# A new order for the first quarter of a fused RWKV and mixture-of-experts kernel, with filler matmuls at other places

## The chip, the cores and the metric

The kernel runs on one core of a Trainium2 chip. Its engines have a queue each: TensorE (PE, with its weight loads as PEld), VectorE (DVE), ScalarE (ACT), GpSimd (POOL), and SyncE (SP), which issues all loads and stores here. The metric is the device time of one execution in microseconds, as the median of several runs.

## The reference

Inputs are `r, k, v, w` of shape (batch 4, heads 8, sequence 768, head size 48), `u` (8 x 48), and the weights of 4 experts (`wq, wk, wv` 384 x 64 each, `wo` 64 x 384) with a gate (384 x 4).

```python
for t in range(S):
    cur = np.einsum('bhd,bhe->bhde', u[None] * kt, vt)
    y[:, :, t] = np.einsum('bhd,bhde->bhe', rt, state + cur)
    state = wt[:, :, :, None] * state + np.einsum('bhd,bhe->bhde', kt, vt)
...
logits = x @ w_gate                       # x: y with the heads side by side (384)
topk = np.argpartition(-logits, K, axis=-1)[..., :K]      # K = 2, softmax over the two: w
for e in range(E):
    q, k, v = x @ wq[e], x @ wk[e], x @ wv[e]
    scores = np.where(causal, -1e9, scale * (q @ k.transpose(0, 2, 1)))
    a = softmax(scores)
    out += (mask of e in topk) * w * (a @ v @ wo[e])
```

## The kernel before

The work is cut into eight units `(b, g)`: batch entry `b`, first or second half `g` of its 768 steps. Each unit has two parts.

`rwkv(b, g)` turns the recurrence into matrix products over chunks of 64 steps. The heads are taken in four pairs. Per pair, the running products of the decays `w` are made by scans on DVE (`suf`, `pre`), after a product of neighbouring decays (`w2`). Keys and rows are scaled with them (`kw`, `rw`, `kt`, `mr`). PE transposes the scaled keys (`ktp`), ACT copies them (`kts`), and PE multiplies them with the values (`ups`). From these the state goes on chunk by chunk, on DVE (`ws`, line 468; the first step of unit 0 on ACT, `us`, line 470). PE also makes the products of keys and rows inside a chunk (`aps`); they are masked with the decay mask `dec_mask` on their way out (`am`). The output `yps` is the sum of both, and DVE adds it into `xn` (`addy`). In unit 0 the term of `u` has its own products: `rkp` on DVE or POOL, and `rkm`, PE products with only two columns. For unit 0 pairs are handled one by one (names with a last digit 0 to 3, or `0000`, `0001`, `0020`, `0021`), for later units two by two.

`moe(b, g)` transposes `xn` (`xp`), makes Q, K and V (`proj`, `vproj`), the scores (`sc`), minimum and exponential (`max` on DVE, `exp` on ACT), the transposes of these (`tp`, `ev`), the product with V (`av`), the gate and the output product.

Every step is one entry that `plan.add` records. Which engine takes a step, and in which order each engine meets its steps, is not found by a scheduler at build time: the string `ORDER` has one word for each step, the engine's letter (A ACT, V DVE, P PE, G POOL, S SP) and the step's number. Each engine runs its words strictly in this order. A load (S) is also made to wait for the last PE step that stands ahead of it in the list, so the list paces the loads.

Among the steps are 94 warming products (numbers 8 to 101, line 1054), matmuls of 128 x 512 bf16 whose result nobody reads. A step whose number stands in no word is left out, so the list also says how many warming products there are and where. Each takes one of the eight PSUM banks (`ps`); PE meets it in order, and it waits until the last reader of the bank's former content is done.

The decay mask and the causal mask are made once, by `masks3` (step V2, lines 329 and 330) and `masks2` (step V3, line 333); `masks4` (V4) makes `tri` and a one-hot table.

## Time and profile before

| | |
|---|---|
| median of 3 runs | 308.04 us (307.08 to 311.17) |
| profiled execution | 308.01 us, span 306.1 us |
| granted PE clock, mean of the span | 0.989 |
| busy share PE, DVE, ACT, POOL | 97%, 81%, 73%, 51% |
| DMA traffic | 44.09 MB, mean 144 GB/s |
| share of PE in the chain that ended last | 93% |

Busy time of PE counts an instruction until its modelled end, so an engine that is always busy may still run at half its clock; the granted clock (1.00 is 2.4 GHz, 0.50 is 1.2 GHz) has to be read beside it. Two per cent of the time are 6.2 us.

### The profile page before, as it was taken

Reading aid. Unit: us, or ns where it says so; the run is one execution under the profiler, and the core shown is the slowest. Engines: PE = TensorE matmul, PEld = TensorE weight load, DVE = VectorE, ACT = ScalarE, POOL = GpSimd, SP = SyncE. Lnnn points to the kernel's source line nnn. Section 1 sums busy time; section 2 is a strip of 40 time slices with the busy share of each in tenths; the row PEclk is TensorE's granted clock in tenths of the full one; section 3 lists DMA queues with packets and bytes.
Section 4 is the critical chain, followed back from the end, with each engine's and each line's share of the span. In section 5 each row is a group of like instructions: output and inputs, shape, how many; then the busy total and the mean of one; then the engine's idle time right before and its main releaser. Section 6 shows DMA issues by size and latency. Waiting matters only on the chain.

```text
span 306.1 us, 12703 instructions
## 1 busy us (share of the span) xinstructions
PE 295.6 (97%) x5216; PEld 245.0 (80%) x5216; DVE 248.1 (81%) x703; ACT 222.0 (73%) x688; POOL 155.3 (51%) x247
## 2 busy tenths in 40 slices
PE   7879999899999999999999999999999999999995
PEld 2669669778886897999789778898889977898784
DVE  5987999989999999989898997978587644687652
ACT  4336399988999889889899867464788656649852
POOL 4848597928556548267787769634211101210510
PEclk9995999999999999999999999999999999999999
DMA  7976785881649763656671573010100000000212
GB/s 227 359 277 216 255 277 167 292 300 43 212 134 329 222 208 117 218 163 207 206 232 77 173 271 107 6 41 24 51 28 2 0 28 28 2 26 2 79 62 94
DMA packets 20073, 44.09 MB, mean 144 GB/s; under 512 B 2352, under 2 KB 10032, under 8 KB 20016
## 3 DMA queue, kind: packets, MB, share of 16 engines
q1 hardware_dynamic: 20016, 43.29, 42.8%
q8 instruction: 41, 0.67, 0.9%
q14 instruction: 16, 0.13, 0.1%
HBM read 38.56 MB, written 4.72 MB: 141 GB/s over the span
## 4 chain that ended last, share of the span: by engine, by line
PE 93%; DVE 3%; issue 1%; DMA 1%; SPq 0%; ACT 0%; DVEq 0%; ACTq 0%
PE ps L779 16%; PE ps L929 13%; PE ps L881 12%; PE ps L1000 9%; PE ps L261 9%; PE ps L817 8%; PE ps L686 5%; PE ps L257 4%; PE ps L399 4%; PE ps L401 4%; PE ps L445 3%; PE ps L772 3%; PE ps L811 1%; DMA lt<-in_wkr_dram 1%; PE ps L978 1%
## 5 line engine op out<-in xcount | busy, mean ns | idle before, releaser
L897 ACT ACTIVATE a<-a,mx 128x128 f32<-128x128 f32 (+5 forms) x96 | 63.8, 667 | 10.0 <-DVE mx L892 9.6
L892 DVE CUSTOM_DVE_ANT_0 a<-ps,causal 128x256 f32<-128x256 f32 (+5 forms) x96 | 56.4, 619 | 12.2 <-PE ps L881 10.8
L265 ACT COPY AT<-ps 128x512 f32<-128x512 f32 (+5 forms) x74 | 38.6, 546 | 10.1 <-PE ps L261 7.9
L929 PE MATMUL ps<-AT,v_sb 128*64 128x384 f32 (+2 forms) x308 | 40.4, 405 | 0.1
L468 DVE CUSTOM_DVE_ANT_0 ys<-ps,ys,suf 112x48 f32<-112x48 f32 x144 | 33.4, 262 | 3.2 <-PE ps L445 0.4
L929 PEld LDWEIGHTS ps<-AT,v_sb 128*64 128x64 f32 x308 | 20.0, 136 | 16.5 <-issue 12.2
L664 ACT ACTIVATE xn<-nat,rk 128x48 f32<-128x48 f32 x126 | 30.5, 326 | 2.0 <-DVE rk L656 1.9
L779 PE MATMUL ps<-xh,wh_qk 128*128 128x384 f32 x84 | 30.4, 362 | 0.0
L881 PE MATMUL ps<-K,Q 64*128 64x384 f32 (+4 forms) x160 | 30.2, 415 | 0.0
L779 PE MATMUL ps<-xl,wh_qk 128*128 128x384 f32 x84 | 28.4, 338 | 0.1
L779 PE MATMUL ps<-xh,wl_qk 128*128 128x384 f32 x84 | 28.3, 336 | 0.0
L989 POOL TENSOR_TENSOR yl<-yr,yh 128x384 fp32r<-128x384 f32 x13 | 13.1, 1010 | 27.5 <-ACT yh L988 26.3
L399 PE MATMUL ps<-vy,am 64*64 64x48 f32 x768 | 25.8, 225 | 1.3 <-issue 1.3
L261 PEld LDWEIGHTS ps<-ident,a 64*128 64x128 f32 x560 | 23.1, 138 | 4.4 <-issue 1.6
L261 PE MATMUL ps<-ident,a 64*128 64x64 f32 x560 | 26.3, 225 | 0.1
L401 PE MATMUL ps<-ys,pre 48*64 48x48 f32 x704 | 25.5, 224 | 0.0
L636 POOL TENSOR_TENSOR kt<-lt,suf 128x768 f32<-128x768 f32 x13 | 21.9, 1685 | 6.3 <-DVE kr L643 3.5
L401 PEld LDWEIGHTS ps<-ys,pre 48*64 48x64 f32 x704 | 22.9, 138 | 2.2 <-DVE wend L464 1.1
L399 PEld LDWEIGHTS ps<-vy,am 64*64 64x64 f32 x768 | 23.5, 139 | 0.1
L638 POOL TENSOR_TENSOR pre<-lt,w 128x768 f32<-128x768 f32 x11 | 18.6, 1690 | 9.6 <-DVE w L630 5.4
L686 PE MATMUL ps<-pre,kt 48*64 48x64 f32 x768 | 18.3, 227 | 1.4 <-issue 0.7
L693 DVE TENSOR_TENSOR am<-ps,dec_mask 64x384 f32<-64x384 f32 (+1 forms) x33 | 18.2, 552 | 1.4 <-PE ps L686 1.0
(173 smaller groups left out, 823.2 us busy)
## 6 DMA issues: line engine op xcount, KB each, us to landing
lt<-in_wkr_dram SPq DMA_DIRECT2D x28, 384.0 KB, 4.4
kr<-in_nat_dram SPq DMA_DIRECT2D x14, 576.0 KB, 4.2
lt<-in_wkr_dram SPq DMA_DIRECT2D x14, 397.0 KB, 4.4
nat<-in_nat_dram SPq DMA_DIRECT2D x16, 288.0 KB, 3.9
vy<-in_vY_dram SPq DMA_DIRECT2D x32, 144.0 KB, 3.7
out_dram<-ob SPq DMA_DIRECT2D x24, 192.0 KB, 1.9
lt<-in_wkr_dram SPq DMA_DIRECT2D x3, 583.0 KB, 5.8
w_qk<-in_wqk_dram SPq DMA_DIRECT2D x1, 768.0 KB, 8.0
```

Of the source, the lines that this page charges most:

```text
L261: nc.tensor.transpose(o()[:, h * 512 + i * 64:h * 512 + i * 64 + 64], src[r], ident[r, r])
L265: nc.scalar.copy(o, i)
L399: nc.tensor.matmul(to, am()[k, c, :], vy()[k, c, :], start=zero and x == 0, stop=i == 2 and x == len(group) - 1)
L401: nc.tensor.matmul(to, pre()[r, c, :], ys()[r, c, :], start=i == x == 0, stop=False)
L468: nc.vector._custom_dve(TENSOR_TENSOR_REDUCE_ADD_MIN, out=new, in0=inc, in1=old, s0=3.0e38, s1=by)
L664: nc.scalar.mul(to[:, i, h, :], v()[:, i, h, :], rk()[:, i, h:h + 1])
L686: nc.tensor.matmul(apss[x]()[half(h if first else h ^ x), c * C:(c + 1) * C], kt()[r, c, :], pre()[r, c, :], start=True, stop=True)
L779: nc.tensor.matmul(pp()[:, 0:384], w[:, qk, k, cs], x()[:, k, :], start=(k == j == 0), stop=(k == j == 2))
L881: nc.tensor.matmul(spv(x)[:, h, :], q_()[p, t], flat(k_())[p, o], start=j == 0, stop=j == len(terms) - 1)
L892: nc.vector.tensor_tensor_reduce(out=a()[:, 0:n].rearrange("p (a n) -> p a n", a=np_), in0=spv(x), in1=causal[:, S - n:S].rearrange("p (a ...
L897: plan.add("exp", {"ACT": t_exp(n)}, lambda e, x=x, y=y, mx=mx, a=a: nc.scalar.activation(a()[:, 0:n], a()[:, 0:n], AF.Exp, bias=mx(), sca ...
L929: nc.tensor.matmul(yp()[e * 64:e * 64 + 64, lo:hi], v_sb()[:, j, ep * 128 + e * 64:ep * 128 + e * 64 + 64], at, start=(j == 0), stop=(j == ...
```

## The change

The change replaces the first two dozen lines of `ORDER`, up to the middle of the first batch entry's second half (the scores of unit `(0, 1)` on PE). From there on the list is as before, but for one load that has another place. Nothing else in the file is touched. All steps of the reference's arithmetic remain. Fourteen steps go to another engine: among them three small copies and a row sum from ACT to DVE, a product of decays of 397 columns from POOL to DVE, one of 576 columns from POOL to DVE, and two of 384 columns from DVE to POOL. Of the warming products 20 stand in the list instead of 21. The first lines of the table, as the diff has them (a row of numbers says little by itself):

```diff
 ORDER = """
-A0 V4 S113 V123 V124 A1 V126 S114 S115 S116 A5 A125 V120 G128 S6 S117 P79 S176 P53 P28 P9 P68 P88 P10 G129 V3 S177 P94
...
+V4 S113 V2 S114 V3 V123 A0 V124 V126 S115 S6 V120 V125 S116 S117 G128 P23 V127 V130 G129 V145 V131 P34 S176 P68 P71
...
```

The queue of PE from its first instructions on. Before, twelve warming products (`causal` is their input) run ahead of the first transposes of keys (`kt000`), then five more and the key sums (`nat000`, `kts0000`), and the products of the `u` term (`rkm`, from `kr000`) come only behind these:

```order
L445 MATMUL ps_68<-nat000_129,kts0000_180 48x48 x12
L1054 LDWEIGHTS causal_69
L1054 MATMUL ps_68<-causal_69 128x512
L570 MATMUL ps_68<-u_t_90,kr000_125 128x2 x3
L257 MATMUL ps_68<-ident_80,kt000_150 128x128 x3
L570 MATMUL ps_68<-u_t_90,kr000_125 128x2 x3
L1054 LDWEIGHTS causal_69
L1054 MATMUL ps_68<-causal_69 128x512
L445 MATMUL ps_68<-nat000_129,kts0001_212 48x48 x12
```

Now four warming products stand ahead of the first `rkm`, then two, and then the transposes, with three more behind them:

```order
L1054 MATMUL ps_68<-causal_69 128x512
L570 MATMUL ps_68<-u_t_90,kr000_124 128x2 x3
L1054 LDWEIGHTS causal_69
L1054 MATMUL ps_68<-causal_69 128x512
L1054 LDWEIGHTS causal_69
L1054 MATMUL ps_68<-causal_69 128x512
L257 MATMUL ps_68<-ident_80,kt000_134 128x128 x3
```

What moved: `rkm` of pair 0 went from behind the second pair's transposes to the front, and eight of the first twelve warming products are gone from there.

The queue of DVE at its start, from the one-hot table on. Before, the masks come late: `causal` behind the first `kr` product, and `dec_mask` only ahead of the scan of the third pair (`w2002`):

```order
L338 TENSOR_SCALAR tri_100<-tri_100 128x16
L578 TENSOR_TENSOR w2000_114<-lt0_66 128x199
L623 SCALAR_TENSOR_TENSOR ps_68<-w2000_114,ps_68 128x198
L628 RECIPROCAL ps_68<-ps_68 128x6
L563 TENSOR_TENSOR kr000_125<-lt0_66 128x2x192
L333 TENSOR_SCALAR causal_69<-d128_78 128x128
L630 SCALAR_TENSOR_TENSOR ps_68<-w2000_114,ps_68 128x198
```

```order
L638 TENSOR_TENSOR pre000_155<-lt0_66,ps_68 128x2x192
L329 TENSOR_SCALAR dec_mask_99<-d128_78 64x64
L330 TENSOR_SCALAR dec_mask_99<-d128_78 64x64
L623 SCALAR_TENSOR_TENSOR ps_68<-w2002_178,ps_68 128x198
L468 ISA ys0000_195<-ps_68,ys0000_195,suf000_123 112x48
```

Now:

```order
L338 TENSOR_SCALAR tri_100<-tri_100 128x16
L329 TENSOR_SCALAR dec_mask_99<-d128_78 64x64
L330 TENSOR_SCALAR dec_mask_99<-d128_78 64x64
L333 TENSOR_SCALAR causal_69<-d128_78 128x128
L578 TENSOR_TENSOR w2000_116<-lt0_66 128x199
L623 SCALAR_TENSOR_TENSOR ps_68<-w2000_116,ps_68 128x198
L628 RECIPROCAL ps_68<-ps_68 128x6
L563 TENSOR_TENSOR kr000_124<-lt0_66 128x2x192
L267 COPY suf000_126<-ps_68 128x6
L630 SCALAR_TENSOR_TENSOR ps_68<-w2000_116,ps_68 128x198
```

What moved: all three mask operations went ahead of the first product of decays (`w2000`), and a copy of six columns came from ACT.

The queue of PE behind the outputs of the first two pairs (`vy0000`, `am0000`), down to the key sums of the fourth pair (`kts0021`). Before, one warming product stands there:

```order
L399 MATMUL ps_68<-vy0000_197,am0000_289 64x48 x4
L1054 LDWEIGHTS causal_69
L1054 MATMUL ps_68<-causal_69 128x512
L257 MATMUL ps_68<-ident_80,xn00_323 128x128 x3
L257 MATMUL ps_68<-ident_80,kt010_350 128x128 x6
L570 MATMUL ps_68<-u_t_90,kr002_363 128x2 x6
L257 MATMUL ps_68<-ident_80,kt002_376 128x128 x3
L445 MATMUL ps_68<-nat010_241,kts0100_380 48x48 x20
L445 MATMUL ps_68<-nat002_217,kts0021_399 48x48 x12
```

Now two stand behind the outputs, and one behind each of the next small groups:

```order
L1054 MATMUL ps_68<-causal_69 128x512
L257 MATMUL ps_68<-ident_80,xn00_311 128x128 x3
L257 MATMUL ps_68<-ident_80,kt010_344 128x128 x6
L1054 LDWEIGHTS causal_69
L1054 MATMUL ps_68<-causal_69 128x512
L570 MATMUL ps_68<-u_t_90,kr002_347 128x2 x3
L1054 LDWEIGHTS causal_69
L1054 MATMUL ps_68<-causal_69 128x512
L257 MATMUL ps_68<-ident_80,kt002_365 128x128 x3
L570 MATMUL ps_68<-u_t_90,kr002_347 128x2 x3
L1054 LDWEIGHTS causal_69
L1054 MATMUL ps_68<-causal_69 128x512
```

What moved: three warming products came in between, the two `rkm` of the second two pairs are parted, and the long key sums of unit `(0, 1)` (`kts0100`) went behind those of the first unit. Three more warming products, where there was one, stand between the `aps` of the first two pairs and their outputs.

## Rows read from the trace of the kernel before

**Rows 1.** Busy time by stretch: stretch, each engine's busy us (records), clock, DMA.
```profile
20.25:23.66 3.41, 3.19 (x84) 2.74 (x84) 3.38 (x9) 2.27 (x7) 1.78 (x3) 1.00 0.30 93
23.66:30.48 6.82, 6.64 (x168) 6.27 (x168) 4.77 (x19) 4.00 (x12) 5.62 (x5) 0.50 0.75 241
30.48:76.00 45.52, 44.50 (x794) 34.73 (x797) 42.01 (x123) 36.18 (x129) 32.43 (x38) 1.00 0.68 224
76.00:306.10 230.10, 226.03 (x3960) 191.89 (x3951) 182.51 (x512) 172.62 (x523) 103.09 (x177) 1.00 0.34 111
```

**Rows 2.** The same view in slices of 1 us, at the clock's two edges.
```profile
23.00:24.00 1.00, 1.00 (x52) 0.89 (x40) 1.00 (x3) 1.00 (x3) 0.49 (x1) 0.83 0.05 17
...
30.00:31.00 1.00, 1.00 (x8) 0.59 (x6) 0.52 (x2) 0.00 (x0) 1.00 (x3) 0.76 0.26 86
```

**Rows 3.** Timeline of PE: start, duration, line, operation [idle before, and its releaser].
```profile
1.42 5.30 PE L1054 MATMUL ps<-causal 128*128 128x512 bf16 x12 [1.42 <-POOL causal L285]
7.38 0.55 PE L257 MATMUL ps<-ident,kt 128*128 128x128 f32 x3 [0.66 <-DVE kt L636]
7.77 1.24 PE L1054 MATMUL ps<-causal 128*128 128x512 bf16 x5
...
10.62 0.73 PE L570 MATMUL ps<-u_t,kr 128*128 128x2 f32 x6
...
11.52 0.48 PE L445 MATMUL ps<-nat,kts 64*48 64x48 f32 x24
...
15.04 0.38 PE L1054 MATMUL ps<-causal 128*128 128x512 bf16 x1 [0.84 <-DVE ys L468]
...
18.57 0.20 PE L399 MATMUL ps<-vy,am 64*64 64x48 f32 x1 [1.28 <-issue]
```

**Rows 4.** Timeline of DVE, the same columns.
```profile
3.41 0.36 DVE L578 TENSOR_TENSOR w<-lt 128x199 f32<-128x199 f32 x1
...
5.49 0.56 DVE L563 TENSOR_TENSOR kr<-lt 128x384 f32<-128x384 f32 x1 [0.81 <-DMA lt<-in_wkr_dram]
5.97 0.22 DVE L333 TENSOR_SCALAR causal<-d 128x128 bf16<-128x128 f32 x1
...
10.10 0.16 DVE L267 COPY suf<-ps 128x6 f32<-128x6 f32 x1
10.17 0.54 DVE L638 TENSOR_TENSOR pre<-lt,ps 128x384 f32<-128x384 f32 x1
10.63 0.67 DVE L329 TENSOR_SCALAR dec_mask<-d 64x64 f32<-64x64 f32 x1
...
11.90 0.57 DVE L623 TENSOR_TENSOR_SCAN ps<-w,ps 128x198 f32<-128x198 f32 x1
...
18.81 0.46 DVE L412 TENSOR_TENSOR xn<-ps,kr 128x288 f32<-128x288 f32 x1 [0.86 <-PE ps L399]
...
23.52 0.55 DVE L634 TENSOR_TENSOR lt<-lt 128x384 f32<-128x384 f32 x1
...
25.68 0.56 DVE L693 TENSOR_TENSOR am<-ps,dec_mask 128x384 f32<-128x384 f32 x1 [0.66 <-PE ps L686]
26.49 0.92 DVE L468 CUSTOM_DVE_ANT_0 ys<-ps,ys,suf 112x48 f32<-112x48 f32 x4 [0.26 <-ACT ys L470]
...
27.89 0.56 DVE L693 TENSOR_TENSOR am<-ps,dec_mask 128x384 f32<-128x384 f32 x1 [0.17 <-PE ps L686]
...
30.48 0.46 DVE L412 TENSOR_TENSOR xn<-ps,kr 128x288 f32<-128x288 f32 x1 [0.82 <-PE ps L399]
...
36.15 0.76 DVE L643 TENSOR_TENSOR kr<-kr 128x576 f32<-128x576 f32 x1
...
36.95 0.81 DVE L656 TENSOR_REDUCE rk<-kr 128x6 f32<-128x288 f32 x2
```

**Rows 5.** Timeline of ACT: the first copy of transposed keys and the first state.
```profile
7.97 0.48 ACT L265 COPY kts<-ps 128x384 f32<-128x384 f32 x1 [3.08 <-PE ps L257]
9.52 0.30 ACT L470 ACTIVATE ys<-ps,suf 112x48 f32<-112x48 f32 x1 [1.08 <-PE ps L445]
```

More of the change, by code (lines that the diff above doesn't have):

```diff
@@ new lines @@
+V146 V148 G142 V147 V149 S177 G150 P121 P94 A122 P100 P133 G151 A134 V152 S119 P88 V153 P83 P56 G184 S118 P135 A136
+V137 S243 V185 V186 P143 P81 V187 A5 A144 V138 G154 P155 P52 V188 V139 P25 S244 A156 S102 G206 P157 A158 V159 S246
+V160 V140 A1 V161 G132 V141 V162 S180 P165 A168 P164 P55 P39 S178 V207 V163 V209 V210 G169 V166 P42 A251 G250 V252 S7
+A274 P173 V174 P170 V171 S245 A208 V253 P41 V254 G255 S292 G257 P73 V203 P237 P265 V181 V211 S179 S107 A105 V213 P96
+P182 A103 A266 G212 V183 V189 P24 G190 A238 P216 V214 P204 V191 G193 V192 A268 P62 A217 V256 G258 G106 S287 P218 A219
@@ new lines @@
+V220 A205 V221 V222 S288 G294 G104 S340 G347 G299 P194 P225 V227 A195 P196 A197 V198 V199 V223 P267 V200 A108 V224
+V201 P226 V229 V202 V275 S289 P231 V232 V276 V269 P234 A215 V235 S247 P967 V295 S248 S249 S341 V296 V270 P241 G300
+S290 A242 P239 A240 V297 V271 V272 P280 V273 S342 V277 V278 A312 P971 V298 P968 P969 V281 A348 V259 V260 V263 A318
+P916 V261 A970 P920 P921 P922 S291 P917 G301 V279 A262 G302 P912 V283 P918 P913 A919 S384 V923 P914 A915 P309 P937
+P946 A310 G352 V349 V350 V351 V940 A941 A392 V938 S386 V949 A950 P311 G353 V947 A264 P955 V313 V319 V956 P944 S385
@@ new lines @@
+V958 V314 A945 V320 P972 V315 V321 V316 G303 V322 G304 V305 V317 A959 V307 G354 S343 P924 P973 A974 S344 P953 G391
+A954 V323 P324 V325 G397 V327 V393 A939 A948 A308 P285 V286 A957 P975 P925 P926 A306 G355 S293 P928 P929 P930 V976
+V394 V395 V356 V357 A931 A927 V932 G933 G396 P960 P962 S437 V358 A963 P951 A952 P331 A332 P362 A363 V360 V978 A961
+G109 S388 V333 S110 P329 P364 V330 P942 P984 V985 A943 A977 V987 S439 A371 V372 V373 S438 P334 A335 V336 P337 A338
+V339 V374 A361 V365 G398 V375 V366 P964 P965 P966 P377 V380 V367 V368 S387 V378 V369 A1005 G399 V400 V444 P980 A988
@@ L1115 @@
+A934 V401 A986 A981 V935 G936 P1033 A359 A979 P1034 V404 P1035 A1036 P1041 P1042 P1043 A1044 P1037 V376 G448 P1038
+P1039 P982 A111 S480 A983 A1040 V402 V370 P993 P989 A990 P991 A992 V996 A997 V994 P1058 P406 V1059 G449 A407 G405
+V1061 V445 S346 A995 V1007 V1008 S390 G1009 V446 S345 S441 S482 S535 P1067 P1000 A1001 G1010 V1070 A1062 V1068 P408
 A415 A409 V410 A403 V416 V411 G112 P1049 P998 A1060 A999 V417 V418 V419 V412 V413 V414 P1050 P1051 A1052 P1045 P1046
-P1047 V447 P1011 P1091 P1092 A1012 A1071 G487 S440 A1048 G452 V420 P1093 A1094 G450 P1013 V1014 A1015 P421 V422 P1074
@@ L1117 @@
[L1117 to L1118 removed]
+P1047 V447 P1011 P1091 P1092 S481 A1012 A1071 G487 S440 A1048 G452 V420 P1093 A1094 G450 P1013 V1014 A1015 P421 V422
+P1074 A1075 V424 P1076 V1077 P1065 A1066 A1069 A1078 V1079 A1080 G1016 P382 V383 V451 V488 V1053 V453 V491 V456 S533
+G492 G1054 S532 G543 V454 V489 G539 P1002 S389 A461 P1003 P1004 A1006 S534 S484 S442 P458 A459 P1072 A1073 P1081 A1082
```

20 lines of the change are left out of this document (removed).

## The prediction

> **What bounds the kernel now.** I read four views in this order: the busy time and granted clock by stretch, the timeline of TensorE (PE) over the first 31 us, the timeline of VectorE (DVE) over the same time, and the timeline of ScalarE (ACT) at the places where it stands between those two.
>
> The stretches [rows 1] say where anything can be won. The order is the old one again from the scores at about 65 us on, and after 76 us PE is busy for 226.03 of 230.10 us at the full clock, so whatever lead or lag PE has there is carried to the end. From 30.48 to 76 us both engines are nearly full: PE 44.50 and DVE 42.01 of 45.52 us. The changed order can therefore hardly pay after 31 us; its room is the ramp before that. There the trace shows three losses.
>
> First, the clock. It goes down at 23.66 us and up again at 30.48 us: the slices around those times show 0.83 and 0.76 as means of the two levels [rows 2], which puts the edges at 0.66 and 0.48 into their microsecond. For 6.82 us PE runs at 1.2 GHz instead of 2.4. It is busy for 6.64 us of that, DVE only for 4.77 [rows 1], and DVE stands waiting for PE's small products four times: 0.66, 0.26, 0.17 and 0.82 us (one of them through ACT), 1.91 us in all [rows 4]. Before the fall PE had run the smallest products of the kernel (3.19 of 3.41 us busy by the records [rows 1], but with matmuls of 2 and 48 columns) after the pauses of 0.84 us at 15.04 and 1.28 us at 18.57 [rows 3].
>
> Second, the decay masks. Two mask operations stand on DVE from 10.63 to 11.90 us, 1.27 us [rows 4], with DVE full before and after; they are what the next state updates wait behind. DVE has a hole of 0.81 us before 5.49, where it waits for the first loads [rows 4].
>
> Third, the pause of 1.28 us inside the output products of the first half [rows 3], released by nothing that the profile names; DVE stands for 0.86 us behind it [rows 4].
>
> **The change part by part.** My sum is against the profiled execution, 308.01 us with a span of 306.10; the median of the three runs is 308.04, so no shift is needed between the two.
>
> *Masks moved to DVE's start.* All three mask operations now stand between the `tri` mask and the first `w2` product. Before, `w2` begins at 3.41 and the work from there to the end of the reciprocal is 1.27 us, then the hole [rows 4]. Now 1.27 us of decay masks and 0.13 us of the causal mask (5.97 to 6.10) come first: `w2` at 4.81, `rkp` at about 6.0 rather than 5.49. The causal mask is gone from behind `rkp` (-0.13), and a copy of 6 columns that ACT made is now there; such a copy takes 0.07 us of DVE's queue (10.10 to 10.17 [rows 4]). So DVE reaches the old place of the decay masks 0.45 us late and saves 1.27 us there. With a second such copy that is a lead of **0.7 us**. If the hole covered everything it would be 1.2; since both numbers are row against row I take 0.7.
>
> *Warming thinned at the start.* Before, 12 warming products run from 1.42 us, 0.42 us apart, which is the 1.2 GHz level for 512 columns; the five behind the first transposes are 0.22 us apart, the 2.4 GHz level [rows 3]. So the first real PE work, at 7.38, ran at full clock. Now four products run (to about 3.3 us), and then PE's queue holds the `rkm` products, which need `rkp`, done at about 6.5. The other warming products stand behind them. PE sits idle for some 3.2 us, where it was warming itself, and meets its first real work at 1.2 GHz. From 6.6 us, with the half-rate cost at twice the full one: `rkm` 1.1 us (0.73 us with its tail at full rate [rows 3], taken as 0.55 without, doubled), two warming products 0.85, transposes 0.8, ACT's copy 0.48 [rows 5], three warming products beside it to 10.7, the key sums `ups` (0.48 us for 24 records at full rate [rows 3]) to 11.1 or 11.5, ACT's first state 0.30 [rows 5]. DVE, which would begin the states at 11.1, begins at about 11.6: 0.5 us lost. The same chain for the second pair is another 0.2 us late if the clock has come up by 10 to 11 us, and about 2.4 us if it has not. I take **-0.7 us**; the ends are 0 (DVE has other work in hand) and -3.
>
> The Trainium skill, "TensorE: Matmul & The Clock Gate", section "What's actually happening", speaks against this part: the throttled state is the default, and activity is what releases it. By that rule the first 5 us of warming products were the price of a ready PE, and taking two thirds of them away puts the release later; the trace agrees in so far as 12 products ran at 1.2 GHz before the rate rose.
>
> *Warming products between aps and ups.* Between the two `aps` of the first pairs and `ups0021`, three products became eight: three behind `aps`, two behind the outputs, one each behind the transposes and the two `rkm`. They take the banks whose last reader is DVE's state or add step, so a product can itself wait: the one at 15.04 waited 0.84 us for DVE's `ys` [rows 3]. Here the ones behind `aps` wait for the end of the state chain of pair 0, which the outputs need anyhow. At full clock each is 0.22 us [rows 3]. Their cover is DVE's queue (3.38 of 3.41 us busy in that stretch [rows 1]); without cover, the three nearest to `ups0021` would cost 0.65 us. I cost them at nothing. What they buy: if the clock stays at 2.4 GHz over 23.66 to 30.48, PE's 6.64 busy us shrink to 3.3, DVE's own 4.77 us become the bound of the stretch, and 6.82 - 4.8 = **2.0 us** are won, which is the sum of DVE's four waits within 0.1. The ends are 0 and 2.0.
>
> *The pause of 1.28 us.* No rule of the order explains it. PE's order has one product fewer, so the same place in its instruction stream now falls behind the outputs. Gain 0 to 0.86 us (DVE's wait [rows 4]); I take **0.3**.
>
> *Loads.* The load issues wait for PE's place in the list. The big weight load now goes ahead of several unit loads, and one piece of the second unit's rows goes behind it; all are needed past 22 us, and DVE shows no wait on a load between 5.49 and 31 us. Nothing on the path, 0 to -0.5.
>
> *Work moved between engines.* After 31 us DVE gains a product of 576 columns (0.76), one row sum (0.40, half of a pair of 0.81) and a product of 397 columns, which I price at that of 384 (0.55), and loses two products of 384 columns (1.10) [rows 4]: +0.6 us. DVE has 3.5 us idle there [rows 1], of which some will take it. ACT and GpSimd get less to do. I take **-0.2**, ends 0 and -0.8.
>
> Sum: 0.7 - 0.7 + 2.0 + 0.3 - 0.2 = 2.1 us. 308.01 - 2.1 = **305.9 us**.
>
> **The rivals.**
>
> *The warming products don't hold the clock.* What decides PE's clock is not shown by busy time: PE was 3.19 of 3.41 us busy just before it fell. The eight products add only 5 x 0.22 = 1.1 us of dense work. For this rival: the small products around them are the same as before. Against it: before, there was one warming product in the 8 us ahead of the fall, now there are five, and DVE's lead pulls the other work closer. Without the 2.0 us the sum is 0.1: **307.9 us**.
>
> *The clock is late, and the kernel is slower.* The place is the first pair of `ups`. If PE is still at 1.2 GHz when `rkm0001`, `ktp0001` and `ups0001` run, the state chain starts some 3 us late instead of 0.7, DVE stalls in front of it, and `aps` and the outputs run at half rate as well. The point that decides is 11 us: up by then, my 0.7 stands; not up, the sum is 0.7 - 3 + 2.0 - 0.2 = -0.5, 308.5 us, and where the later products then don't hold the clock either, -2.5, **310.5 us**. The Trainium skill, same page, section "What you observe", has the rise move by half a microsecond from run to run, so runs of one kernel may fall on both sides of such a point. For it: PE's idle 3.2 us are new. Against: from 6.6 us PE is packed.
>
> *The lead is given back.* From 31 to 76 us DVE is 92% busy and gets 0.6 us more work. If each piece of it falls before something PE needs, and the loads of the second unit come no earlier (they are released by buffers, not by PE), 1.5 of the 2.1 us go: **307.4 us**.
>
> **How the numbers follow.** Forecast 0.52 (by its terms at their ends 304.4, with 0.7 + 2.0 + 0.86 and no loss at the start, to 307.0, with a loss of 1.5 there and nothing from the pause), no hold 0.20, late clock and slower 0.12, given back 0.14, other 0.02. The range runs from 303.8 (everything at its good end, and a little more) to 309.4, which leaves out the worse half of the late clock. Two per cent, about what a measurement of this kernel can tell from no change, are 6.2 us. To be faster by that, all three losses of the ramp and more would have to vanish: 0.03. Slower by that takes a late clock that lasts beyond the outputs and then falls again: 0.04. Within: 0.93.
>
> **What would show it.** Right: the granted clock at full from about 11 us on without the hole at 24 to 30 us; PE idle from 3.3 to 6.5 us; the two decay masks at about 3.5 to 4.8 us on DVE; the first key transposes later than 7.38, above 8 us; the first `proj` about 2 us before its old 30.3 us, and the same lead at 76 us. Wrong: a hole in the clock anywhere before 31 us; a wait of over 1 us of DVE on ACT's states at 11 to 15 us; a lead at 31 us that is gone at 76; or a stall of the first loads, since the order of their issues is new.

## The result, and the profile after

The changed kernel takes 311.14 us (median of 22 runs, 308.33 to 314.47) where the kernel before takes 309.10 (22 runs beside it, 306.69 to 315.15). The ratio is **1.0085, with an interval of 1.0060 to 1.0111**: slower by about 2.6 us, where 2.1 us less were forecast, and outside the range. The ratio leaves out runs in a slow state, those over 1.5% above the fastest of their kernel; over all runs the medians differ by 2.0 us. The difference is below two per cent, but its interval is clear of one. The profiled execution of the changed kernel took 314.38 us (span 312.6, mean clock 0.984) and was among the slowest of its runs, so its times tell where time can go, not how much goes there as a rule.

Three numbers carried the forecast: a fall of the clock at 23.66 us that would not come, a thinned start that would cost 0.7 us, and loads that would cost nothing. The same views of the changed kernel first. The stretches (busy time of PE, PEld, DVE, ACT, POOL, then clock, DMA share and GB/s):

```profile
20.05:23.37 3.32, 1.48 (x9) 0.88 (x9) 3.29 (x6) 1.66 (x4) 2.60 (x2) 1.00 0.75 234
23.37:33.61 10.24, 10.24 (x188) 9.21 (x190) 6.13 (x20) 5.13 (x16) 7.61 (x7) 0.50 0.63 206
33.61:93.90 60.29, 58.44 (x1192) 45.23 (x1186) 54.78 (x163) 45.96 (x147) 38.67 (x49) 1.00 0.69 211
93.90:312.60 218.70, 214.21 (x3621) 182.94 (x3619) 171.44 (x480) 161.39 (x495) 96.28 (x166) 1.00 0.34 107
```

and the slices at the two edges of the clock:

```profile
23.00:24.00 1.00, 1.00 (x7) 0.88 (x7) 0.90 (x3) 0.45 (x2) 0.02 (x1) 0.68 0.81 306
...
33.00:34.00 1.00, 1.00 (x53) 1.00 (x48) 0.60 (x3) 0.53 (x3) 0.90 (x2) 0.70 0.03 13
```

The means of 0.68 and 0.70 put the edges at about 23.37 and 33.61 us. In this execution the clock falls at 23.4 us all the same, and for 10.24 us where it was 6.82 [rows 1]; PE has only 1.48 us of work in the 3.32 us ahead of the fall, where it had 3.19 of 3.41. The last stretch begins at the first output product, 93.90 us, which was at 87.46 before. From there to the end PE runs the same 3621 matmuls in 218.70 us as before in 218.64 (306.10 - 87.46): between these two executions nothing is lost or won in the unchanged part, and the 6.4 us by which this one is late are all there by then. (It isn't always so: a later execution of the changed kernel takes 221.5 us from there to the end.)

The timeline of PE (start, duration, line, operation, [idle before, and its releaser]):

```profile
1.42 1.89 PE L1054 MATMUL ps<-causal 128*128 128x512 bf16 x4 [1.42 <-POOL causal L285]
6.11 1.44 PE L570 MATMUL ps<-u_t,kr 128*128 128x2 f32 x6 [2.80 <-DVE kr L563]
...
8.22 0.85 PE L257 MATMUL ps<-ident,kt 128*128 128x128 f32 x3
8.86 1.49 PE L1054 MATMUL ps<-causal 128*128 128x512 bf16 x3
...
10.94 1.44 PE L570 MATMUL ps<-u_t,kr 128*128 128x2 f32 x6
...
14.77 2.39 PE L686 MATMUL ps<-pre,kt 48*64 48x64 f32 x48
17.09 0.82 PE L1054 MATMUL ps<-causal 128*128 128x512 bf16 x3
...
22.80 1.05 PE L257 MATMUL ps<-ident,kt 128*128 128x128 f32 x6 [1.75 <-POOL kt L636]
```

PE stands for 2.80 us in front of the first `rkm`, and works at half rate from there: the six small products take 1.44 us at 6.11 and again at 10.94 (0.73 before [rows 3]). At 17.09 three warming products take 0.82 us, which is full rate. The granted clock reads 1.00 over these half-rate products as well, as the profile has no value for it before its first rise; the start's clock has to be read from durations. The new place of idleness is 22.80: the transposes of the second half wait 1.75 us for GpSimd's `kt`. The first `proj` comes at 35.08, where it was 30.3.

The timeline of DVE:

```profile
3.40 0.18 DVE L329 TENSOR_SCALAR dec_mask<-d 64x64 f32<-64x64 f32 x1
3.60 0.19 DVE L330 TENSOR_SCALAR dec_mask<-d 64x64 f32<-64x64 f32 x1
...
8.66 0.37 DVE L578 TENSOR_TENSOR w<-lt 128x199 f32<-128x199 f32 x1 [1.26 <-DMA lt<-in_wkr_dram]
...
15.35 0.92 DVE L468 CUSTOM_DVE_ANT_0 ys<-ps,ys,suf 112x48 f32<-112x48 f32 x4 [1.46 <-ACT ys L470]
...
29.04 0.88 DVE L468 CUSTOM_DVE_ANT_0 ys<-ps,ys,suf 112x48 f32<-112x48 f32 x3 [1.36 <-ACT ys L470]
```

and of ACT, the first copy of transposed keys and the first state:

```profile
9.10 0.48 ACT L265 COPY kts<-ps 128x384 f32<-128x384 f32 x1 [1.35 <-PE ps L257]
...
11.04 0.30 ACT L470 ACTIVATE ys<-ps,suf 112x48 f32<-112x48 f32 x1 [1.46 <-DVE ps L630]
```

The two decay masks take 0.18 and 0.19 us at the start, 0.40 from the first's begin to the next operation, and not the 1.27 that they took in the middle [rows 4]. The DVE time saved comes back as waits: 1.26 us for a load at 8.66 (in two later executions DVE takes this step at 7.42 and 7.71 without a wait), 1.46 and 1.36 for ACT's first states, which stand behind PE's half-rate products. ACT's first state comes at 11.04 instead of 9.52 [rows 5].

The mean clock of a whole execution says how long it ran at half rate after the first rise (not where, and not how long the start was at half rate), and each run has it. For the 105 runs of the kernel before that stood beside the experiments (five chips) and the 22 of the changed kernel, in groups by that mean clock (median time in us, number of runs):

| mean clock | half rate for some | before | changed |
|---|---|---|---|
| 0.998 to 1.000 | 0 us | 307.8 (19) | none |
| 0.992 to 0.995 | 4 us | 308.0 (24) | 311.1 (15) |
| 0.986 to 0.989 | 7 us | 308.6 (19) | none |
| 0.981 to 0.984 | 11 us | 310.6 (18) | 312.3 (7) |
| 0.976 to 0.978 | 14 us | 311.5 (14) | none |
| 0.967 to 0.973 | 17 us | 312.1 (11) | none |

(The second column is twice what is missing to 1, times 308 us.) Three things are to be read here. By this mean the changed order holds the clock better: its median is 0.994, that of before 0.989, though none of the 22 runs is without half rate and 19 of the 105 are. But at the same mean clock it is **3.1 us slower** (a late rise at the start, which the mean leaves out, can be part of that), and runs of the order before with 7 us of half rate take 0.8 us more than those with none (1.1 by the means, give or take 0.8), not 2.0. The price is not even: from 7 to 14 us it is 2.9 us more.

### The profile page after: what moved, and what is told of

Same layout as the page of the kernel before. It is cut to its first block, busy times and chain, and to the rows that moved or that the text cites. A ratio compares the mean times of both kernels' runs of the same rounds, so it can differ in the third digit from the quotient of the medians.

```text
span 312.6 us, 12701 instructions
## 1 busy us (share of the span) xinstructions
PE 300.1 (96%) x5214; PEld 248.7 (80%) x5214; DVE 249.2 (80%) x707; ACT 220.0 (70%) x673; POOL 154.9 (50%) x247
## 4 chain that ended last, share of the span: by engine, by line
PE 85%; POOL 5%; DVE 3%; DMA 3%; issue 2%; SPq 0%; ACT 0%; POOLq 0%; DVEq 0%; ACTq 0%
PE ps L779 15%; PE ps L929 13%; PE ps L881 12%; PE ps L261 9%; PE ps L1000 9%; PE ps L817 8%; PE ps L686 4%; PE ps L257 3%; PE ps L399 3%; PE ps L445 3%; PE ps L401 3%; DMA kr<-in_nat_dram 2%; POOL kt L636 2%; PE ps L570 2%; DMA lt<-in_wkr_dram 1%
## 5 line engine op out<-in xcount | busy, mean ns | idle before, releaser
L265 ACT COPY AT<-ps 128x640 f32<-128x640 f32 (+5 forms) x75 | 39.0, 541 | 12.8 <-PE ps L261 10.5
L779 PE MATMUL ps<-xh,wh_qk 128*128 128x384 f32 x84 | 30.4, 362 | 0.0
L261 PE MATMUL ps<-ident,a 64*128 64x64 f32 x564 | 27.0, 225 | 1.6 <-DVE mx L892 0.9
L779 PE MATMUL ps<-xh,wl_qk 128*128 128x384 f32 x84 | 28.2, 336 | 0.0
L399 PE MATMUL ps<-vy,am 64*64 64x48 f32 x768 | 25.1, 221 | 0.3 <-DMA vy<-in_vY_dram 0.3
L401 PE MATMUL ps<-ys,pre 48*64 48x48 f32 x704 | 24.6, 220 | 0.0
L401 PEld LDWEIGHTS ps<-ys,pre 48*64 48x64 f32 x704 | 22.0, 135 | 1.7 <-issue 1.4
L399 PEld LDWEIGHTS ps<-vy,am 64*64 64x64 f32 x768 | 22.7, 135 | 0.5 <-DMA vy<-in_vY_dram 0.4
L841 POOL TENSOR_TENSOR ge<-v_sb,m 128x12 f32<-128x12 f32 x8 | 1.7, 209 | 36.7 <-DVE c L837 33.9
```

What stands on the lines that cost most here:

```text
L261: nc.tensor.transpose(o()[:, h * 512 + i * 64:h * 512 + i * 64 + 64], src[r], ident[r, r])
L265: nc.scalar.copy(o, i)
L399: nc.tensor.matmul(to, am()[k, c, :], vy()[k, c, :], start=zero and x == 0, stop=i == 2 and x == len(group) - 1)
L401: nc.tensor.matmul(to, pre()[r, c, :], ys()[r, c, :], start=i == x == 0, stop=False)
L779: nc.tensor.matmul(pp()[:, 0:384], w[:, qk, k, cs], x()[:, k, :], start=(k == j == 0), stop=(k == j == 2))
```

## The experiments

The kernels are made by moving words of `ORDER`; S243 and S244 are the loads of decays and keys for the second half of the first batch entry, P26 and the like warming products. A diff shows the words around an edit. Each ratio is to the kernel before on the same chip.

**Which part of the order loses.** Up to V235 (about 30 us) the changed order, then the old one, and the reverse (one load, S292, stands later in the first of the two):

```diff
 P231 V232 V276 V269 P234 A215 V235
-S247 P967 V295 S248 S249 S341 V296
+S249 A295 G300 V270 V277 S248 S247
```
```diff
 V276 V232 A215 P234 V235
-V277 S248 S247 V271 G347
+S292 G347 S247 P967 S248 S341 V296
```

> The changed order up to the last output sum of the first unit (one load of values left for later), then the old order. If the ramp makes the loss, 1.5 to 3 us above the old kernel, as the changed one. If the order after 31 us makes it, the old kernel's time or up to 2 us below.

> The old order up to the last output sum of the first unit (about 31 us in the old kernel), then the changed order. If the ramp makes the loss, the time is the old kernel's within 0.5 us. If the changed order after 31 us makes it, 1.5 to 3 us above the old kernel.

Measured: the changed ramp with the old rest 312.63 us, **1.0159 [1.0092, 1.0225]**; the old ramp with the changed rest 309.04, **1.0027 [0.9991, 1.0062]**. The loss is in the ramp; what is behind it costs little or nothing. The trace of the first shows something that the profile of the changed kernel doesn't have, a pause inside the second outputs (PE timeline):

```profile
32.79 0.20 PE L399 MATMUL ps<-vy,am 64*64 64x48 f32 x1 [2.74 <-issue]
32.92 0.59 PE L772 MATMUL ps<-xh,w_qk 128*128 128x384 f32 x1
```

Its clock was at full from 17 us on; from 34.0 to 37.4 us it is at half.

**The changed kernel twice more.** No edit.

> The changed kernel once more, for a second trace. By the late clock: aps at 1.2 GHz (about 2.4 us), first outputs at about 17.5 us instead of 15.4. By the fetch of PE's instructions: where the granted clock doesn't fall at 24 us, the second outputs run at full rate and PE then stands 2 to 3 us inside them without any releaser, with one packet of the instruction queue in flight, and the clock falls behind that.

> The changed kernel a third time. Of the first two traces one had aps in 2.39 us (1.2 GHz) and 314.4 us in all, one had them in 1.59 and 306.95 us. By the late clock this one is decided at the same place: aps in about 2.4 us goes with first outputs at 17.5 us or later and 309 us or more, aps in 1.6 with outputs at 15.3 and about 307.

Measured: 306.95 us (before on that chip 308.39) and 316.11 (309.92). The first of them has no half rate behind its start, and its start is not late: the 48 `aps` come at 13.04 and take 1.59 us, where they came at 14.77 and took 2.39. It is the nearest to what the forecast described, and at 306.95 us it is 1.0 us above the forecast; but it is one of 24. The third has `aps` at 13.16 as well, where about 307 us was expected of that, then a wait of 2.00 us for `kt` and half rate from 20.7 to 30.9 (its timeline of PE):

```profile
20.93 1.33 PE L257 MATMUL ps<-ident,kt 128*128 128x128 f32 x5 [2.00 <-POOL kt L636]
```

Three executions of one program thus differ by 9 us. They differ most in the ramp: late start or not, wait for `kt` of 0.59, 1.75 or 2.00 us, clock held or not; their first output products come at 86.41, 93.90 and 92.81 us. The third loses 2.8 us more behind that, with a pause of PE of 1.45 us at 156.43 and half rate from 157.2 to 160.6.

**The early masks alone**, in the order before:

```diff
-A0 V4 S113 V123
+A0 V4 V2 V3 S113 V123
...
-P10 G129 V3 S177 P94
+P10 G129 S177 P94
...
-S243 S244 V2 P57 G184
+S243 S244 P57 G184
```

> The old order with the three mask operations moved to the start of VectorE's queue, all else the same. My prediction's term: VectorE is 0.7 us earlier at the first states; the time falls by 0.3 to 1 us. If the pause inside the first outputs and the late loads set the pace of the ramp, the lead is gone by 20 us and the time is the same within 0.4 us.

Measured: 310.73 us, **1.0083 [1.0041, 1.0124]**. Not a gain but a loss. In its trace the first transposes wait 1.44 us for `kt` (0.66 before; but the same wait is 1.44 to 2.27 us in five traces whose masks stand as before, so it isn't the masks that make it) and the clock is at half for 13.65 us (its stretches):

```profile
19.25:32.90 13.65, 13.47 (x255) 12.38 (x254) 9.33 (x30) 6.71 (x18) 9.48 (x9) 0.50 0.56 181
```

Eight of its twelve runs have a clock of 0.971 to 0.978. The masks are free where they now stand, and the time they leave does not come out at the end.

**The thinned start alone**, six of the twelve first warming products taken from the order before:

```diff
-P68 P88 P10 G129 V3 S177 P94
+P68 P88 G129 V3 S177
...
-S180 S119 P21 V127 P86 V130 P34 P90 V145
+S180 S119 V127 V130 V145
```

> The old order with six of its first twelve warming products taken out, all else the same. By the late clock: PE stands idle from about 4.2 to 7.4 us, the first transposes and key sums run at 1.2 GHz, and the time is 0.5 to 2 us above the old kernel (half of the warming is left). If the start of the clock doesn't matter because VectorE has other work, within 0.3 us of the old kernel.

Measured: 310.42 us, **1.0043 [0.9995, 1.0090]**. PE is idle for 3.24 us in front of the first transposes, and in this trace the first outputs begin at 19.53 us instead of 15.35. Its mean clock reads 1.000, but PE is at half rate until about 23 us; the second key sums, for instance, take 0.73 us where they took 0.48 [rows 3] (timeline of PE):

```profile
14.91 0.73 PE L445 MATMUL ps<-nat,kts 64*48 64x48 f32 x24
```

The time, then, is 0.4% longer with an interval that just holds no change.

**Filling the start of the changed kernel**: eight more warming products ahead of the first `rkm`, and the same with eight later ones taken away:

```diff
-V147 V149 S177 G150 P121 P94
+V147 V149 S177 G150 P9 P10 P20 P21 P28 P53 P79 P86 P121 P94
```
```diff
-S119 P88 V153 P83 P56 G184
+S119 P88 V153 G184
...
-S292 G257 P73 V203
+S292 G257 V203
```

> The changed order with eight more warming products in front of its first rkm, so that twelve run before PE's first real work as in the old kernel. If the changed kernel loses its time because PE meets its first key sums at 1.2 GHz, the aps of the first pairs take 0.9 us instead of 2.4, the first outputs start 1.5 to 2.5 us earlier, and the time falls by 1.5 to 2.5 us against the changed kernel, to about the old kernel's or up to 1 us below it. If the loads' places or the order after 31 us make the loss, the first outputs come earlier but the time stays about 0.8% above the old one.

> The changed order with twelve warming products in front and eight of the later ones taken out, so 20 in all as in the changed kernel: PE's stream has the same number of instructions from the first outputs on. By the late clock, and if the extra 16 instructions were what lost the time in the kernel with 28 products (pauses without a releaser at other places of the later stream): first outputs at about 15 us and 306 to 308 us, 0 to 1% below the old kernel. If twelve products in front are bad for another reason: 311 us or more as with 28.

Measured: 314.49 us, **1.0185 [1.0114, 1.0257]**, and 315.96, **1.0191 [1.0115, 1.0267]**. Filling the start does bring the first outputs to 14.91 and 13.91 us (17.84 in the profile after), and the kernel is slower all the same. With the later products the clock is at full until 31.1 us, and falls there behind a pause of PE of 2.94 us inside the second outputs; without them it falls at 17.8. So the later products do hold the clock, as forecast, and the first ones bring the start forward; neither pays. The second stream isn't quite as long as that of the changed kernel, as was meant: nine transposes of 128 columns became 18 of 64 (5223 matmuls for 5214).

**The held clock alone**: six warming products between 20 and 28 us in the order before.

```diff
-V211 P265 P204 V213 G212 V189 A266 P182 A183
+V211 P265 P23 P204 P24 V213 G212 V189 A266 P182 P25 A183
...
-A205 P216 G190
+A205 P216 P26 G190
...
-P267 P218 A219
+P267 P29 P218 P30 A219
```

> The old order with six warming products among the small products between the first and the second outputs, all else the same. If warming products there hold the clock and the clock is what costs the 6.8 us at half rate, no half rate shows at 24 to 30 us and the time falls by 1.5 to 2 us. If PE's instruction fetch is the next bound, the clock holds, a pause of 2 to 3 us stands inside the second outputs, and the time is the same or up to 1 us above.

Measured: 309.76 us, **1.0052 [1.0005, 1.0099]**. In the very stretch of [rows 1] the clock is at full:

```profile
23.66:30.48 6.82, 6.26 (x198) 5.03 (x197) 5.21 (x23) 4.29 (x12) 5.98 (x5) 1.00 0.74 248
```

PE gets through 198 matmuls where it got through 168 [rows 1], and the first `proj` comes at 29.27 instead of 30.3. DVE, though, gains only 0.44 busy us (5.21 to 4.77), and from the end of the first outputs to the first `proj` it is 11.18 us for 11.53; the rest of the earlier `proj` is the pause of 1.28 us [rows 3], which this trace doesn't have. No pause stands in its second outputs either. The unchanged part takes 220.6 us in it for 218.6. This is the term of 2.0 us by itself, and it does not make the kernel faster; what six products more cost in the stream behind the ramp was not measured apart.

**The late loads.** In the order before, S243 and S244 put where the change puts them, and in the changed order put early (run twice, on two chips):

```diff
-G151 V147 V153 S243 S244 V2 P57 G184 A134 P135 V185
+G151 V147 V153 V2 P57 G184 A134 P135 S243 V185
...
-P143 A144 P155 A156
+P143 A144 P155 S244 A156
```
```diff
-G184 S118 P135 A136 V137 S243 V185
+G184 S118 S243 S244 P135 A136 V137 V185
...
-V139 P25 S244 A156
+V139 P25 A156
```

> The order before, with the two loads of the first unit's second half (S243, S244) paced as the change paces them: the first behind the transposes of the second pair, the second behind the first state sums of the second pair. Theory that late loads hold GpSimd's kt and so PE's transposes at 20 us: PE idle of 0.5 to 2 us ahead of those transposes, ratio 1.002 to 1.007, more if the clock falls behind it. Rival (the loads are needed past 22 us and cost nothing): no idle over 0.3 us there and a ratio of 0.998 to 1.002.

> The changed order with the two loads of the second unit (decays and keys) issued ahead of the first key sums, as in the old order, instead of behind them. If these late loads make the loss (POOL's kt is late and PE waits 0.6 to 1.75 us for it at 20 to 23 us), the wait goes and the time falls by 0.6 to 1.7 us. If the late clock sets the pace, the wait shrinks but the time stays within 0.5 us of the changed kernel, about 0.8% above the old one.

> loads_after once more, beside fetch_free on the same chip. Theory that the late loads make about half of the loss: ratio 1.001 to 1.006 again and no idle over 0.7 us ahead of the transposes of the second half. Rival (its first result was chance): 1.006 to 1.011 as the changed kernel.

Measured: late in the order before 312.10 us, **1.0084 [1.0039, 1.0129]**. Two words make as much of a loss as the whole change. The trace has the chain. First the timeline of GpSimd, whose product `lt` waits for the load, with `kt` behind it:

```profile
18.15 0.93 POOL L632 TENSOR_TENSOR lt<-lt 128x384 f32<-128x384 f32 x1 [2.71 <-DMA lt<-in_wkr_dram]
19.16 1.68 POOL L636 TENSOR_TENSOR kt<-lt,suf 128x768 f32<-128x768 f32 x1
```

Then the timeline of PE, which waits for `kt`:

```profile
20.89 0.87 PE L257 MATMUL ps<-ident,kt 128*128 128x128 f32 x6 [1.16 <-POOL kt L636]
```

and the stretches around it, in the second of which the clock is down (from 22.66 us; it was down from 15.83 to 19.25 as well, ahead of this wait):

```profile
20.05:22.17 2.12, 1.28 (x12) 1.28 (x13) 2.09 (x4) 0.66 (x3) 0.89 (x2) 1.00 0.77 275
22.17:32.90 10.73, 10.55 (x242) 9.57 (x242) 7.43 (x25) 5.80 (x16) 8.57 (x9) 0.52 0.53 157
```

Of its ten runs nine have a clock of 0.972 to 0.978. Early in the changed order, the same loads cut PE's wait for `kt` from 1.75 to 0.55 us in both traces, and the clock is held past 31 us; the times are 310.91 us, 1.0037 [0.9989, 1.0084], and 312.30, 1.0101 [1.0059, 1.0143]. The two together can't be told from the changed kernel's own 1.0085. One loss is smaller and another is met in its place, a pause of PE (timeline of loads_again):

```profile
29.65 0.27 PE L399 MATMUL ps<-vy,am 64*64 64x48 f32 x4
32.55 0.20 PE L399 MATMUL ps<-vy,am 64*64 64x48 f32 x1 [2.63 <-issue]
```

and in the stretches the clock falls right behind it:

```profile
30.00:32.60 2.60, 0.05 (x1) 0.00 (x0) 0.12 (x1) 0.36 (x2) 2.60 (x3) 1.00 0.45 170
32.60:36.00 3.40, 3.40 (x29) 2.28 (x32) 2.93 (x11) 0.93 (x3) 1.99 (x3) 0.53 0.46 134
```

**What the pause is.** The page lists the DMA queues (packets, MB, share of 16 engines):

```profile
q8 instruction: 41, 0.67, 0.9%
```

These 41 packets of 16 KB are as many as PE's 5214 matmuls and 5214 weight loads make if one packet holds 254 of them. By windows of 0.2 us I took the time at which each packet runs and the number of PE's records (matmuls and weight loads) begun by then; the table has the packet nearest the second outputs (DMA share over the 1.5 us ahead of it):

| kernel | packet at us | PE records by then | DMA share | pause there, us | clock behind it |
|---|---|---|---|---|---|
| w12_after | 28.2 | 948 | 0.95 | 2.94 | falls |
| after_then_before | 30.4 | 948 | 0.91 | 2.74 | falls |
| loads_again | 30.0 | 951 | 0.97 | 2.63 | falls |
| loads_after | 29.4 | 951 | 1.01 | 2.54 | falls |
| half_free | 29.2 | 879 | 0.85 | 1.70 | falls |
| w12_fill | 28.0 | 808 | 1.00 | 0.70 | holds |
| after_again | 26.6 | 770 | 1.10 | 0.71 | holds |
| weights_late | 26.8 | 764 | 1.09 | 0.61 | holds |
| after_third | 31.6 | 822 | 0.85 | 0.84 | holds |
| pad8_before | 29.2 | 906 | 0.99 | 1.78 | holds |
| thin_before | 31.0 | 864 | 1.01 | 0.31, behind them | holds |
| fetch_free | 27.6 | 732 | 0.00 | none | holds |
| before | 26.0 | 730 | 0.88 | none | at half already |

The later in PE's stream the packet comes, the longer the pause as a rule (thin_before is the exception, where the outputs were through before PE ran dry); at 948 to 951 PE has run dry before it is there. In all eleven with a pause PE goes on 1.3 to 1.5 us behind the packet's end (a packet takes some 0.95 us). The DMA share doesn't order the pauses: it is about 1 ahead of the shortest and of the longest. Four kernels of the table are experiments on this.

*Eight more products ahead of the second outputs* (added to the kernel with the filled start):

```diff
-V202 V275 S289 P231 V232
+V202 V275 S289 P26 P27 P29 P30 P31 P32 P33 P35 P231 V232
```

> The changed order with twelve warming products in front and eight more (1.7 us) ahead of the second outputs. If PE's pause of 2.9 us inside these outputs is the fetch of its next 256 instructions, the pause shrinks by about 1.7 us to 1.2, the clock need not fall behind it, and the time is the same as without the eight or up to 2 us less. If the pause is a wait for data or for a bank, it stays at 2.9 and the time grows by 1.7 us.

Measured: the pause shrinks from 2.94 to 0.70 us and no fall follows; the time is 317.07 us, **1.0289 [1.0223, 1.0356]**, for a reason that comes below.

*The load traffic taken away*: in the changed kernel with early loads, four loads and the three GpSimd products beside them, or the last two loads and two of the products, moved behind the second outputs.

```diff
-G106 S287 P218
+G106 P218
...
-V222 S288 G294 G104 S340 G347 G299 P194
+V222 G104 P194
...
-V275 S289 P231
+V275 P231
...
-V269 P234 A215
+V269 P234 S287 S288 G294 S340 G347 G299 S289 A215
```
```diff
-G104 S340 G347 G299 P194
+G104 P194
...
-V275 S289 P231
+V275 P231
...
-V269 P234 A215
+V269 P234 S340 G347 G299 S289 A215
```

> The changed kernel with early loads (loads_after), and four loads of the next batch entry with their three GpSimd products moved from just ahead of the second outputs to just behind them. Theory that PE's pause of 2.54 us in the second outputs is a packet of its instruction stream waiting among load traffic: with the traffic gone the pause falls below 1 us, no clock fall follows it, the first projection comes at 29.5 to 30.5 instead of 32.05 us, ratio 0.992 to 1.000 unless the late loads cost it back after 35 us. Rival (PE's small products simply use up its instructions faster than packets come, whatever the loads do): the pause stays at 2 us or more and the ratio at 1.003 or above.

> The changed kernel with early loads, and only the last two of four big loads (with the GpSimd steps between them) moved behind the second outputs. Theory that the pause there follows the traffic: the packet comes at a PE record below 900 instead of 951, the pause is 0 to 1.5 us instead of 2.5 to 2.6, and as the decay product of the next unit keeps its load, no wait of 4 us follows; ratio 0.994 to 1.003. Rival: the pause stays above 2 us, or DVE's wait comes all the same; ratio 1.004 to 1.012.

Measured: with all four away the pause is gone, and the first `proj` comes at 30.27 instead of 32.05 and 32.68; with two away it is 1.70 us. The first is no clean pair, since its clock was at half for 3.4 us ahead of the outputs, so PE came to them more slowly; the second has the clock at full until then, and the size of the pause between the two ends (timeline of half_free). That the traffic is what makes the packet late rests on this one pair of traces.

```profile
31.67 0.20 PE L399 MATMUL ps<-vy,am 64*64 64x48 f32 x1 [1.70 <-issue]
```

The times: 313.23 us, 1.0119 [1.0052, 1.0185], since the four late loads are paid at 39.59 us (its timeline of PE; a product of decays on GpSimd is late, DVE waits 4.67 us for it, and PE for DVE),

```profile
39.59 0.80 PE L811 MATMUL ps<-w_vg,xh 128*128 128x260 f32 x1 [4.11 <-DVE am L693]
```

and 310.82 us, **1.0041 [1.0000, 1.0082]**, with the first run of early loads the best of the changed ramp. Nine of its ten runs have a clock of 0.998 to 1.000, and still they take 310.8 us, 3 us more than the order before at that clock.

*The same in the order before*, whose pause of 1.28 us at 18.57 [rows 3] has a packet at 16.2 us and 353 records: three weight loads (1.35 MB) moved behind the first outputs.

```diff
-V161 P165 S102 A168 G169 V207 V162 A208 S7 S107 V140
+V161 P165 A168 G169 V207 V162 A208 V140
...
-V174 P170 S249
+V174 P170 S102 S7 S107 S249
```

> The order before, with the three weight loads issued at 13.6 to 15.4 us (1.35 MB) moved behind the first outputs (18.5 us). Theory that the pause of 1.28 us at 18.57 is an instruction packet among load traffic: the DMA share over 15 to 17 us falls well below the 1.0 of before, the packet comes at a lower count of PE's records than 353, the pause shrinks below 0.6 us, ratio 0.993 to 1.000. Rival (the pause is set by PE's own pace, or the weights, read from 23.0 us on, then come late): pause of 1 us or more, or the first projection later than before, ratio 1.000 to 1.008.

Measured: the packet comes at 268 records and the pause is 0.72 us, but the DMA share ahead of it is 0.98 still, so the traffic just ahead of it hadn't gone, and the run doesn't say what moved the packet. The time is 311.06 us, 1.0063 [1.0022, 1.0105]; this trace has another pause of 1.68 us at 152.53, in the unchanged part.

**A longer stream.** Eight tiny products (32 x 2) in the order before, at its start, and behind the ramp, where they came to stand at 60.8 to 62.7 us (beside the words, the size of these eight products is changed):

```diff
-V145 V131 P133
+V145 V131 P26 P29 P30 P32 P33 P35 P36 P37 P133
```
```diff
-V380 V400 P1033
+V380 V400 P8 P11 P12 P13 P14 P15 P16 P17 P1033
```

> The old order with eight tiny products (32 x 2, two instructions each) where PE waits 0.66 us ahead of its first transposes: the same work, but every later instruction of PE stands 16 further in its stream. If the pauses without a releaser come from where the blocks of 256 instructions end, they move to other places and the time changes by 1 to 6 us though nothing else does. If the place in the stream doesn't matter, within 0.5 us of the old kernel.

> The order before with eight tiny products (32 x 2) added at about 75 us, behind the ramp. Theory that a longer PE stream moves the packets' borders into places where PE runs out of instructions: time in which PE waits for nothing named, after 80 us, rises from 0.3 to 2 us or more, ratio 1.006 to 1.014. Rival (the length is harmless, the added products of the earlier runs cost by their place in the ramp): at most 0.8 us of such time, ratio 0.999 to 1.004.

Measured: 314.46 us, 1.0155 [1.0077, 1.0233], and 315.93, **1.0161 [1.0065, 1.0256]**. The first is no clean test, as its products waited 2.50 us for a bank in the ramp. The second leaves the order of the ramp as it was; its products waited 1.14 us for ACT to be done with a bank, and in this trace the clock is at half from 62.4 to 69.3 us, so it isn't quite clean either. In both, PE waits behind 80 us for nothing that the trace names, for instance in the timeline of pad8_late:

```profile
177.94 0.40 PE L261 MATMUL ps<-ident,a 64*128 64x64 f32 x6 [1.03 <-issue]
```

Summed over PE's timeline from 80 us on, this time is 0.33 us in the kernel before, 3.5 and 3.4 in these two; 5.25 with eight products more in the changed kernel (w12_after) and 6.44 with sixteen (w12_fill). Traces of programs with 5214 to 5216 matmuls have 0.24 to 3.0 (the changed kernel 1.66, 0.41 and 2.70 in its three), so a single trace says little, but all four with eight products or more added are beyond them, and so is front12_after with its nine (3.81). The time from the first output product to the end says the same: 217.8 to 221.5 us in the traces of the old length, 221.2 to 223.4 in the three with eight more, 222.2 in front12_after, and 226.1 with sixteen. For pad8_late the 1.14 us of the bank and 3.0 us more of this time, from its one trace, are 4.1 beside the 5.0 us that the ratio says; what the half rate there costs comes on top and isn't known. It fits, too, that w12_after and w12_fill were slower whatever they did in the ramp: what w12_fill won there was lost later.

## Why the prediction was wrong

*What bounds the kernel.* Right that all room is in the ramp, and that a lead or lag at its end is carried: the unchanged part is equal to 0.1 us in the two profiled executions, though it varies by 3.7 us over all traces of this length. Three of the four signs of being wrong are in the profile: a hole in the clock, a wait of 1.46 us on ACT's states, a stall of 1.26 us on a first load. But the row of before on which all was built, 6.82 us of half rate with four waits of DVE, was taken for a loss of 2 us without asking what the kernel gains if it goes.

*Warming products hold the clock, +2.0.* **The failed step.** The mechanism is as the forecast has it: without the later products the clock falls at 17.8 (front12_after), with six of them in the order before it is at full over the whole stretch (hold_before), and the changed kernel's median clock is 0.994 against 0.989. The price was wrong. The runs of before at full clock are 0.8 us faster than those with 7 us of half rate, hold_before wins 0.35 us from the end of the first outputs to the first `proj`, and as a whole it is 0.5% slower. The forecast took DVE's busy time for the next bound (4.77 us of 6.82) and forgot PE's stream: where PE comes to the second outputs at full rate, the packet of its instructions can be late, PE stands for up to 2.9 us, and behind the four pauses of 2.5 us and more the clock falls (behind 1.70 once, behind 1.78 not). This pause is seen in four traces with the changed ramp (loads_after, loads_again, after_then_before, and w12_after with a filled start), and at 1.70 us in half_free, but not in the three of the changed kernel itself (0.71 in after_again). The 15 runs of 22 with a clock of 0.993 to 0.994 may have it, as loads_again (0.995) and after_then_before (0.994) have it with just this clock; but no such run was traced, and hold_before and weights_late have this clock by a fall at 7.5 us.

*Loads, 0 to -0.5.* Wrong. I wrote that nothing is needed before 22 us and that DVE shows no wait on them. It isn't DVE that waits but GpSimd: it begins `lt` for the second half at 15.10 us in the kernel before. late_before, which moves only S243 and S244, costs 0.84%. In the changed order, moving them back gains less (1.0037 and 1.0101 against 1.0085), and the pause comes instead.

*Warming thinned, -0.7 with ends 0 and -3.* Too small, and the rival was right in kind. Its worse case, a late clock that falls again, gave 310.5 us, 2.5 above before, and the profiled run has both; that the median lies 2.0 above is in part luck, as the other two traces have no late start. PE's idle time was forecast well (3.2 us, 2.80 measured), the first key transposes above 8 us too (8.22). In five of the eight traces with this start (the three of the changed kernel, the two with early loads, fetch_free, half_free, after_then_before) the first outputs begin at 17.2 to 18.1 us, in three at 15.3 to 15.4. In the seven traces with the old first transposes and all twelve products ahead of them they begin at 14.9 to 16.4, 15.8 on the mean, so the thinned start costs either nothing or some 2 us, 1.0 on the mean (16.8 for the eight). The deciding point, 11 us, was passed in the profiled run with `rkm` at half rate (1.44 us at 10.94). Its price of 3 us is about what was seen (1.46 us of DVE at 15.35, `aps` 0.8 us longer).

*Masks, +0.7.* The three mask operations cost 0.55 us at the start (the next one begins at 3.95), less than the 1.4 that I charged, so DVE was further ahead than forecast, and ended in a wait of 1.26 us for the next load. Early masks alone make the kernel 0.8% slower; the trace gives a longer half-rate stretch as the way, but why earlier masks bring it was not settled.

*The pause of 1.28 us, +0.3.* It does go away at the first outputs of the changed kernel, as forecast, and turns up in the second ones.

*Work between engines, -0.2.* before_then_after has 1.0027 with an interval that holds both no change and this term's 0.2 us; nothing speaks against it.

At equal mean clock the changed kernel is 3.1 us behind. Of these the late start is about 1.0, and a pause of 2.6 in place of one of 1.28, if it is there, is 1.3; both are put together from different traces, so they are estimates to their order only, and some 0.8 us are left without a name. In the run traced at 0.984 the late load, the wait for `kt` and a long fall of the clock take the place of the pause. That the loss is in the ramp is shown; how it divides is argued, as no single step taken back brings the old time. By their medians no version here beats the kernel before.

## What to carry to other kernels

Before a stretch at half clock is priced as a loss, look at several runs of the same kernel sorted by their mean clock: their own scatter says about what such a stretch is worth, and here it was 0.8 us of a supposed 2.0. The mean says neither where the half rate lies nor how late the first rise is, so it takes traces beside it. In a list that paces loads by the order of another engine, moving a load means to follow each of its readers on every engine, GpSimd too, to the first one that could begin. And a gain in the pace of tiny matmuls has to be checked against PE's instruction stream: filler products make it longer for the whole program.

## What had not been expected of the hardware

PE's instructions come in packets of 16 KB (41 of them, 0.67 MB) by a DMA queue beside that of the loads, and where one comes late PE pauses for nothing that the profile names; the longest pauses, of 2.5 to 2.94 us, are in a block of 48-column products, where PE begins 85 matmuls in 1.30 us (28.00 to 29.30 us of loads_after). PE goes on 1.3 to 1.5 us behind the end of the packet that it lacked, in every trace with such a pause in or right behind the second outputs. The Trainium skill, "Runtime: NRT & Kernel Launch", section "Instruction fetch mechanics", has each engine fetch its own stream in blocks of 16 KiB (256 instructions) through a DMA queue while it executes, and calls the cost mostly hidden. The traces agree on the blocks (254 by the count above). On the cost they do not: beside load traffic, in a block of tiny products at the full clock, it is up to 2.94 us at one place.

Eight matmuls of 32 x 2 added to some 5200, behind the ramp, cost 1.6% [0.65, 2.56], of which their own wait for a bank is 1.14 us; a fall of the clock at that wait, seen in the one trace, is in it too.

In the first microseconds the granted clock reads 1.00 while products of 512 columns take 0.42 us each, the 1.2 GHz level (and 24 key sums 0.73 us instead of 0.48, up to 14.25 us in the profile after and 14.91 us in thin_before). There the durations of equal products show PE's clock, and the clock column doesn't.
